# Where the plain part's last product stands, and which words and sums take a PSUM bank

## The chip, the cores and the metric

The kernel runs on one core of one Trainium2 chip. The metric is the device time of one execution in microseconds (us). Before the change it is 564.85 us, the median of three runs (564.38 to 565.11).

## The reference

The program chains three blocks in 32-bit floats. First a decaying linear attention over 2 batches, 8 heads, 768 positions and head size 64, in blocks of 64 positions with a running state. Its result, 1536 tokens by 512 features, goes through two feed-forward layers:

```python
rms = np.sqrt(np.mean(x * x, axis=-1, keepdims=True) + 1e-06)
xn = x / rms * rms_g
g = xn @ w_gate                                   # 512 x 1536
val = xn @ w_val                                  # 512 x 1536
x = (g * (1.0 / (1.0 + np.exp(-g))) * val) @ w_out            # 1536 x 512
h = np.maximum(np.maximum(x @ w1, x @ w2), x @ w3)            # 512 x 768 each
out = h @ w_out2                                  # 768 x 512
```

## The kernel before

**Split numbers.** Every operand of a large matmul is held as two parts, a high one (`wh`, `xh`, `hh`) and the remainder (`wl`, `xl`, `hl`). One product of a 128 x 128 weight tile with 512 columns is three matmuls: high by high, high by low, low by high.

**Tiles.** The 1536 tokens are three blocks of 512 columns, j = 0, 1, 2. Each weight unit is 128 x 512 words: `("g", f)`, `("v", f)` and `("o", f)` for hidden tile f = 0 to 11 of the first layer, `("1", f)`, `("2", f)`, `("3", f)` and `("p", f)` for f = 0 to 5 of the second.

**Two ways of multiplying.** Hidden tiles f = 0 to 5 are the plain part: `first_stage` goes through (group, j, f) in 18 steps, each with `hidden1` (gate and value products, 24 matmuls) and then `finish`, the output product of the step before, delayed by one step: four acc banks, 12 matmuls in `out1`, and at the last f of a group `drain1` (L456), four VectorE adds that bring the banks into `acc_sb`. From f = 6 on, `second_stage` computes the three column blocks by a scheme of fewer products: sums and differences of quarters of the inputs (names `s1` to `s4`, `11`, `12`, `22`, `2`) are multiplied by weight units and by pair sums of them. A work list names its pieces as `(at, n)`. `piece` makes 6 matmuls for one of them in tile p, q, r or p2, and `out_pair` 6 for an output tile acc. The `finish` of the last plain step is left over by the first stage and stands in this list: between `(at, (0, 1))` and `(at, 2)` of f = 6.

**The weight pipeline.** Raw words come by DMA on SP's queue (L149). A unit is made in cycles of three turns (`third_of_unit`), and `gap()`, called after each piece and twice in `finish`, makes one turn. Turn 0 begins a new unit (`begin_unit`: the load of a later one, two ScalarE passes L227 and L228, tile W) and makes the first step of the unit begun before: L188, VectorE, into tile `mid`. Turn 1 finishes the unit before that (cast to `wh` on ScalarE, L157; `wl` on GpSimd, L160) and makes L191 on `mid`. Turn 2 makes L194 on VectorE and L196 on GpSimd, which brings the result into W. `mid` is W itself in the first stage and a PSUM bank in the second.

**Pair sums.** A key with T (`("Tg", f)`, `("Tv", f)`, `("T1", f)` and so on) is a unit made from two finished ones, without a load. The first of a pair (`first_sum`) needs a copy of its partner's words in a PSUM bank, tile `tsum` (L181, ScalarE). Four half-width VectorE subtractions (L203) turn W and tsum into both sums. The second (`second_sum`) is finished straight from tsum: cast L157, and `wl` by VectorE, L173. The copy is made by `copy_partner` in turn 1 of the cycle ahead of that of the subtractions, which are spread over turns 0, 1 and 2 of their cycle as 2, 1, 1.

**Banks and order.** One pool of eight PSUM banks serves acc, p, q, r, p2, mid, tsum and the tiles of the first stage. A new tile takes the bank that was released first in program order, and waits for that bank's last reader. Each engine runs its instructions in the order of the program text; the kernel has no planner (`manual_schedule`).

**Quarter sums.** After the last output products of block j = 1 in the first layer, `sums_of_quarters` makes the second layer's inputs from the acc banks: two groups of VectorE L540, ScalarE casts L547, VectorE and GpSimd L447. It sets `quiet`, and no turn of the weight pipeline runs until `loud` in the work list, which stands after the output products of block j = 2 and the first pieces of the second layer.

Of the kernel before, what the change touches and what calls it, by code (L numbers as in the profile page):

```python
# [9 lines left out]
F32 = mybir.dt.float32  # L10
# [16 lines left out]
def tile_decay_attention_swiglu_maxout(  # L27
# [112 lines left out]
    mid = {}  # L140
    sums_in = {}
    room = [WBUFS, 8]
    pos = {"load": 0, "made": 0, "raw": 0, "step": 0, "gap": 0, "quiet": False, "lag": 3}

    def load_to(n):
        while pos["load"] < min(n, len(raw_list)):
# [5 lines left out]

    def finish_unit(key, W, at):
        if key:
            wh = wpools[at].tile([P, 512], F32R, tag="wh", name="wh")
            wl = wpools[at].tile([P, 512], F32R, tag="wl", name="wl")
            nc.scalar.copy(out=wh, in_=W.bitcast(F32))  # L157
            if second_sum(key):
                return lambda: lower_of_sum(key, W, wh, wl)
            nc.gpsimd.tensor_tensor(out=wl, in0=W.bitcast(F32), in1=wh.bitcast(F32), op=ALU.subtract)  # L160
            units[key] = (wh, wl)

    def first_sum(key):
        return key and (key[0] == "Tg" or key[0] != "Tv" and key[0][0] == "T" and key[1] % 2 == 0)

    def second_sum(key):
        return key[0][0] == "T" and not first_sum(key)

    def partner(key):
        return ("v", key[1]) if key[0] == "Tg" else (key[0][1], key[1] + 1)  # L170
# [2 lines left out]
        nc.vector.tensor_tensor(out=wl, in0=W.bitcast(F32), in1=wh.bitcast(F32), op=ALU.subtract)  # L173
        units[key] = (wh, wl)

    def copy_partner():
        if stage1 and first_sum(stage1[-1][0]):
            other = partner(stage1[-1][0])
            if other not in sums_in:
                sums_in[other] = psum.tile([P, 512], I32, tag="bank", name="tsum")  # L180
                nc.scalar.copy(out=sums_in[other].bitcast(F32), in_=words[other].bitcast(F32))  # L181

    def words_of_unit(n, key, W, at, lo, hi):

        if key and lo is not None:
            if n == 0:
                mid[key] = W if pos["step"] < len(steps) else psum.tile([P, 512], I32, tag="bank", name="mid")
                nc.vector.tensor_scalar(out=mid[key].bitcast(F32), in0=W.bitcast(F32), scalar1=LEAST, scalar2=MOST,  # L188
                                        op0=ALU.max, op1=ALU.min)
            elif n == 1:  # L190
                nc.vector.tensor_scalar(out=mid[key], in0=mid[key], scalar1=0x07FFFFFF, scalar2=3,  # L191
                                        op0=ALU.bitwise_and, op1=ALU.logical_shift_left)
            else:
                nc.vector.scalar_tensor_tensor(out=W, in0=hi, scalar=-0x40000000, in1=mid.pop(key),  # L194
                                               op0=ALU.bitwise_and, op1=ALU.bitwise_or)
                nc.gpsimd.tensor_tensor(out=W, in0=W, in1=lo, op=ALU.add)  # L196
        elif first_sum(key):
            a, b = W.bitcast(F32), sums_in[partner(key)].bitcast(F32)
            kept = words[partner(key)].bitcast(F32)
            todo = ((a[:, :HF], b[:, :HF], a[:, :HF]), (b[:, :HF], b[:, HF:], kept[:, :HF]),  # L200
                    (b[:, HF:], b[:, HF:], a[:, :HF]), (a[:, HF:], a[:, HF:], b[:, HF:]))
            for o, x, y in todo[(0, 2, 3)[n]:(2, 3, 4)[n]]:
                nc.vector.tensor_tensor(out=o, in0=x, in1=y, op=ALU.subtract)  # L203

    def begin_unit():
        if pos["made"] == len(unit_list):
            return
        key = unit_list[pos["made"]]
        at = group_of[key] % 2
        if first_use[key] <= pos["step"] + (6 if pos["step"] < 18 else 9) and at < len(wpools) and (key is None or room[at]):  # L210
            pos["made"] += 1
            if key is None:
                stage1.append((None,) * 5)
                return
            room[at] -= 1
            held[key] = at
            if key[0][0] == "T":
                stage1.append((key, (sums_in if second_sum(key) else words)[key[0][1], key[1]], at, None, None))
                return
            load_to(pos["raw"] + (3 if pos["step"] else 1))  # L220
            pos["raw"] += 1
            t = raws.pop(key).rearrange("p k (f w) -> p (k f) w", w=2)
            lo, hi = t[:, :, 0], t[:, :, 1]
            spare = key[0] in "12" and key[1] % 2
            W = (lates[0] if spare else wp).tile([P, 512], I32, tag="W", name="W", bufs=1 if spare else 3)
            words[key] = W
            nc.scalar.activation(out=W.bitcast(F32), in_=hi.bitcast(F32), func=AF.Abs)  # L227
            nc.scalar.activation(out=lo, in_=lo.bitcast(U32), func=AF.Copy, scale=2.0 ** -29)  # L228
            stage1.append((key, W, at, lo, hi))
# [14 lines left out]
    def third_of_unit():  # L244

        if not thirds:
            done = stage2.pop(0) if stage2 else (None,) * 3
            unit = stage1.pop(0) if stage1 else (None,) * 5
            later = []
            thirds.extend([lambda: (begin_unit(), words_of_unit(0, *unit)),  # L250
                           lambda: (later.append(finish_unit(*done)), copy_partner(), words_of_unit(1, *unit)),
                           lambda: (later[0] and later[0](), words_of_unit(2, *unit), stage2.append(unit[:3]))])
        thirds.pop(0)()

# [579 lines left out]
            third_of_unit()  # L834

    def second_stage(finish):
        def loud():
            pos["quiet"] = False
            third_of_unit()


        work = []
        before = None
        for f in range(PLAIN, F1):
            at = f, None
            outs = [[], [], []]
            if f == PLAIN:
                outs[1] = [finish]
            elif (f - PLAIN) % 2 == 0:
                outs = [out_block(f - 2, j) for j in (0, 2, 1)]  # L850
            work.append((at, 1))
            if before:
                work.append((before, 4))
            before = at
            if f == F1 - 1:
                work += [(at, n) for n in (5, 6, (0, 0), 2, 7, 3, (0, 1), (1, 0), 4)]
            else:
                work += [(at, 5), (at, (0, 0))] + outs[0] + [(at, 6), (at, (0, 1))] + outs[1] + [(at, 2)] + outs[2]
                work += [(at, n) for n in (3, 7, (1, 0), (1, 1))]
        first, second, third = (0, 0), (0, 1), (0, 2)  # L860
        work += out_block(F1 - 2, 0) + [(at, (1, 1))] + out_block(F1 - 2, 1) + [(first, 1), (first, 2), (second, 1)]
        work += out_block(F1 - 2, 2) + [loud]
        work += [(first, n) for n in (5, 6)] + [(second, 2)] + [(first, n) for n in (3, 7, (0, 0), (0, 1), (1, 0), 4, (1, 1))]
        work += [(second, n) for n in ((0, 0), (0, 1), 5, (1, 0), 6, 3, 7)] + [(third, 1), (second, (1, 1)), (second, 4)]
        work += [(third, n) for n in (2, (0, 0), (0, 1), (1, 0), 5, (1, 1), 6, 3)]
        at = 1, 0
        work += [(at, 1), (third, 7), (at, 2), (at, (0, 0)), (third, 4)] + [(at, n) for n in ((0, 1), 5, (1, 0), (1, 1), 6, 3)]
        outs = [lambda j=j, t=t: out2(0, j, t) for j in range(NBLK) for t in range(NB // P)]
        work += outs[:2] + [(at, 7)] + outs[2:4] + [(at, 4)] + outs[4:]
        before = None  # L870
        for g in range(F2 // 2):
            for i in range(3):
                at = g, i
                if at <= (1, 0):
                    continue
                if before:
                    work += [(at, 1), (before, 4)]
                else:
                    work.append((at, 1))
                work += [(at, n) for n in (5, (0, 0), 6, (0, 1), 2, 3, 7, (1, 0), (1, 1))]  # L880
                before = at
                if g and i == 0:
                    outs = [lambda g=g, j=j, t=t: out2(g - 1, j, t) for j in range(NBLK) for t in range(NB // P)]
                    work += outs[:2] + [(at, 4)] + outs[2:]
                    before = None
        work.append((before, 4))
        work += [lambda g=F2 // 2 - 1, j=j, t=t: out2(g, j, t) for j in range(NBLK) for t in range(NB // P)]
        for w in work:
            if callable(w):
                w()  # L890
            else:
                piece(*w)
# [66 lines left out]
```

## Time and profile before

| | before |
|---|---|
| median of three timed runs | 564.85 us |
| the profiled execution | 567.43 us |
| its span, first to last instruction | 564.5 us |
| TensorE matmuls (PE) | 547.1 us busy, 97%, 2880 |
| VectorE (DVE) | 383.1 us, 68%, 583 |
| GpSimd (POOL) | 320.7 us, 57%, 256 |
| ScalarE (ACT) | 272.0 us, 48%, 517 |
| mean granted TensorE clock | 0.989 |

The profile is of one execution. Times in rows are us from the start of the span. A row of the timeline gives start and duration, engine, line, operation, the tile written <- the tiles read, shapes, and in brackets how long the engine stood idle before it and whose end released it. Matmuls are pipelined, so their durations overlap, and the distance of their starts tells the pace. A granted clock of 1.00 is 2.4 GHz, 0.50 is 1.2 GHz.

### The profile page before, as it was taken

The numbers are of one execution on the slowest core, as the hardware profiler recorded it, in microseconds if no ns is written. First come the engines' busy times: TensorE is split into PE (matmuls) and PEld (weight loads), VectorE is DVE, ScalarE is ACT, GpSimd is POOL, SyncE is SP. The second block draws the span as 40 slices with busy tenths as digits, with TensorE's granted clock in tenths as the row PEclk, the third lists the DMA queues.
The fourth block names the chain that finished last, engine by engine and source line by source line (L and its number), as shares of the span: only waits on it lengthen the run. The fifth ranks groups of instructions, "written<-read, shape, count | busy, mean of one in ns | idle before, by whom it ended". The sixth has DMA issues, their size and how long they took to land.

```text
span 564.5 us, 7794 instructions
## 1 busy us (share of the span) xinstructions
PE 547.1 (97%) x2880; PEld 452.0 (80%) x2880; DVE 383.1 (68%) x583; ACT 272.0 (48%) x517; POOL 320.7 (57%) x256
## 2 busy tenths in 40 slices
PE   7979989999999999989999999999999999999997
PEld 7968767888788888778888888878888888888885
DVE  6687997423358789686676867896567567774364
ACT  3566754332354534446626455555465755552120
POOL 2577998311167677647727747687377553962050
PEclk9998999999999999989999999999999999999999
DMA  8767646000023211212312222120222322210014
GB/s 204 189 177 188 176 134 168 1 0 1 2 81 107 72 40 35 66 48 76 113 38 74 75 74 76 37 75 1 74 75 76 96 91 75 74 39 0 2 45 178
DMA packets 64646, 44.54 MB, mean 79 GB/s; under 512 B 39264, under 2 KB 60768, under 8 KB 64608
## 3 DMA queue, kind: packets, MB, share of 16 engines
q1 hardware_dynamic: 63936, 44.05, 26.6%
q8 instruction: 22, 0.36, 0.3%
q14 instruction: 16, 0.13, 0.1%
q10 hardware_dynamic: 672, 0.01, 0.1%
HBM read 40.90 MB, written 3.15 MB: 78 GB/s over the span
## 4 chain that ended last, share of the span: by engine, by line
PE 83%; DVE 9%; DMA 2%; ACT 2%; issue 1%; POOL 1%; SPq 0%; ACTq 0%; DVEq 0%
PE p L637 27%; PE r L637 7%; PE acc L425 5%; PE acc L427 5%; PE acc L426 5%; PE q L637 4%; PE acc L820 3%; PE acc L819 3%; PE acc L821 3%; PE pg L425 3%; PE pg L426 3%; PE pg L427 2%; PE pv L425 2%; PE pv L427 2%; PE pv L426 2%; PE px L322 2%
## 5 line engine op out<-in xcount | busy, mean ns | idle before, releaser
L160 POOL TENSOR_TENSOR wl<-W,wh 128x512 fp32r<-128x512 f32 x75 | 102.8, 1371 | 43.4 <-ACT wh L157 43.3
L196 POOL TENSOR_TENSOR W<-W,wraw 128x512 int32<-128x512 int32 x60 | 80.7, 1346 | 72.6 <-DVE W L194 70.8
L157 ACT CAST wh<-W 128x512 fp32r<-128x512 f32 x75 | 46.5, 620 | 68.0 <-POOL W L196 67.8
L439 POOL TENSOR_TENSOR hl<-sg,hh 128x512 fp32r<-128x512 f32 x36 | 48.8, 1356 | 43.5 <-ACT hh L438 43.5
L425 PE MATMUL acc<-hh,wh 128*128 128x512 f32 x144 | 57.2, 397 | 1.0 <-DVE xl L447 1.0
L426 PE MATMUL acc<-hl,wh 128*128 128x512 f32 x144 | 56.2, 390 | 0.0
L427 PE MATMUL acc<-hh,wl 128*128 128x512 f32 x144 | 56.1, 390 | 0.0
L637 PE MATMUL p<-xl,wh 128*128 128x512 f32 x120 | 46.7, 389 | 0.0
L637 PE MATMUL p<-xh,wh 128*128 128x512 f32 x120 | 46.7, 389 | 0.0
L637 PE MATMUL p<-xh,wl 128*128 128x512 f32 x120 | 46.7, 389 | 0.0
L227 ACT ACTIVATE W<-wraw 128x512 f32<-128x512 f32 x60 | 40.0, 667 | 9.6 <-POOL wl L160 5.6
L438 ACT CAST hh<-sg 128x512 fp32r<-128x512 f32 x36 | 22.3, 620 | 43.6 <-DVE sg L572 37.4
L228 ACT ACTIVATE wraw<-wraw 128x512 int32<-128x512 uint32 x60 | 39.7, 661 | 0.0
L439 POOL TENSOR_TENSOR hl<-m,hh 128x512 fp32r<-128x512 f32 x18 | 24.5, 1366 | 24.2 <-ACT hh L438 24.1
L637 PE MATMUL p<-yh,wh 128*128 128x512 f32 x90 | 35.0, 389 | 0.0
L637 PE MATMUL p<-yl,wh 128*128 128x512 f32 x90 | 35.0, 389 | 0.0
L637 PE MATMUL p<-yh,wl 128*128 128x512 f32 x90 | 35.0, 389 | 0.0
L692 ACT COPY c<-p 128x512 f32<-128x512 f32 x30 | 17.7, 588 | 33.5 <-PE p L637 33.4
L425 PEld LDWEIGHTS acc<-hh,wh 128*128 128x128 f32 x144 | 27.0, 188 | 7.5 <-DVE xl L447 1.8
L792 DVE TENSOR_TENSOR acc_sb<-acc,acc_sb 128x512 f32<-128x512 f32 x34 | 23.3, 690 | 14.1 <-PE acc L427 13.3
L188 DVE TENSOR_SCALAR mid<-W 128x512 f32<-128x512 f32 x37 | 25.4, 686 | 9.3 <-ACT W L227 4.7
L427 PEld LDWEIGHTS acc<-hh,wl 128*128 128x128 f32 x144 | 27.0, 188 | 5.8
(177 smaller groups left out, 1444.2 us busy)
## 6 DMA issues: line engine op xcount, KB each, us to landing
wraw<-in_moe_w_out_dram SPq DMA_DIRECT2D x18, 512.0 KB, 3.4
wraw<-in_moe_w_dram SPq DMA_DIRECT2D x18, 512.0 KB, 3.6
wraw<-in_moe_w_gate_dram SPq DMA_DIRECT2D x12, 512.0 KB, 3.6
wraw<-in_moe_w_val_dram SPq DMA_DIRECT2D x12, 512.0 KB, 3.6
kn<-in_k_dram SPq DMA_DIRECT2D x12, 256.0 KB, 4.1
qn<-in_q_dram SPq DMA_DIRECT2D x12, 256.0 KB, 4.4
vn<-in_v_dram SPq DMA_DIRECT2D x12, 256.0 KB, 4.7
out_dram<-acc_sb SPq DMA_DIRECT2D x12, 256.0 KB, 2.0
```

The source lines that it names most:

```text
L157: nc.scalar.copy(out=wh, in_=W.bitcast(F32))
L160: nc.gpsimd.tensor_tensor(out=wl, in0=W.bitcast(F32), in1=wh.bitcast(F32), op=ALU.subtract)
L188: nc.vector.tensor_scalar(out=mid[key].bitcast(F32), in0=W.bitcast(F32), scalar1=LEAST, scalar2=MOST, op0=ALU.max, op1=ALU.min)
L196: nc.gpsimd.tensor_tensor(out=W, in0=W, in1=lo, op=ALU.add)
L227: nc.scalar.activation(out=W.bitcast(F32), in_=hi.bitcast(F32), func=AF.Abs)
L228: nc.scalar.activation(out=lo, in_=lo.bitcast(U32), func=AF.Copy, scale=2.0 ** -29)
L425: nc.tensor.matmul(out=out, lhsT=wh, rhs=xh_, start=first, stop=False)
L426: nc.tensor.matmul(out=out, lhsT=wh, rhs=xl_, start=False, stop=False)
L427: nc.tensor.matmul(out=out, lhsT=wl, rhs=xh_, start=False, stop=last)
L439: nc.gpsimd.tensor_tensor(out=dst_l, in0=src, in1=dst_h.bitcast(F32), op=ALU.subtract)
L637: nc.tensor.matmul(out=ps, lhsT=w[:, ks], rhs=r[:, o + k, :], start=first and k == 0 and n == 0, stop=k == 1 and n == 2, skip_group_check= ...
L792: nc.vector.tensor_tensor(out=ps if kept else y, in0=ps, in1=y, op=ALU.add)
```

## The change

Three things change. The leftover `finish` stands ahead of `(at, (0, 1))` of f = 6 instead of behind it. `mid` stays W until the new work item `wide`, right after that piece, where before it became a bank at the beginning of the second stage. And the copy of a partner into tsum is made by `sum_bank` in turn 0 of the pair's own cycle, where before it was made two turns earlier; the four subtractions are spread over the turns as 0, 2, 2, and the second sum looks up its tile when it is finished instead of when it is begun.

```diff
     def finish_unit(key, W, at):
         if key:
+            if second_sum(key):
+                W = sums_in.pop((key[0][1], key[1]))
...
-    def copy_partner():
-        if stage1 and first_sum(stage1[-1][0]):
-            other = partner(stage1[-1][0])
-            if other not in sums_in:
-                sums_in[other] = psum.tile([P, 512], I32, tag="bank", name="tsum")
-                nc.scalar.copy(out=sums_in[other].bitcast(F32), in_=words[other].bitcast(F32))
+    def sum_bank(key):
+        other = partner(key)
+        sums_in[other] = psum.tile([P, 512], I32, tag="bank", name="tsum")
+        nc.scalar.copy(out=sums_in[other].bitcast(F32), in_=words[other].bitcast(F32))
...
-                mid[key] = W if pos["step"] < len(steps) else psum.tile([P, 512], I32, tag="bank", name="mid")
+                mid[key] = W if pos["narrow"] else psum.tile([P, 512], I32, tag="bank", name="mid")
...
         elif first_sum(key):
+            if n == 0:
+                sum_bank(key)
+                return
...
-            for o, x, y in todo[(0, 2, 3)[n]:(2, 3, 4)[n]]:
+            for o, x, y in todo[2 * n - 2:2 * n]:
                 nc.vector.tensor_tensor(out=o, in0=x, in1=y, op=ALU.subtract)
...
-                           lambda: (later.append(finish_unit(*done)), copy_partner(), words_of_unit(1, *unit)),
+                           lambda: (later.append(finish_unit(*done)), words_of_unit(1, *unit)),
...
+        def wide():
+            pos["narrow"] = False
...
             if f == PLAIN:
-                outs[1] = [finish]
+                work += [(at, n) for n in (1, 5, (0, 0), 6)] + [finish, (at, (0, 1)), wide]
+                work += [(at, n) for n in (2, 3, 7, (1, 0), (1, 1))]
+                before = at
+                continue
```

## Rows read from the trace of the kernel before

**Rows 1.** The page: busy us, share of the span, instructions of TensorE.
```profile
PE 547.1 (97%) x2880; PEld 452.0 (80%) x2880; DVE 383.1 (68%) x583; ACT 272.0 (48%) x517; POOL 320.7 (57%) x256
```

**Rows 2.** Stages from the seam on: length, engines' busy us, granted clock, DMA.
```profile
239.70:241.70 2.00, 0.04 (x1) 0.00 (x0) 1.32 (x3) 2.00 (x5) 1.19 (x2) 1.00 0.30 123
241.70:245.50 3.80, 3.78 (x10) 2.97 (x11) 2.77 (x5) 1.03 (x3) 0.52 (x1) 0.55 0.00 0
245.50:374.00 128.50, 128.50 (x568) 106.21 (x566) 95.49 (x151) 66.20 (x121) 80.96 (x62) 1.00 0.22 70
374.00:382.00 8.00, 7.01 (x30) 5.32 (x30) 7.84 (x14) 7.12 (x15) 7.08 (x6) 1.00 0.21 67
382.00:545.00 163.00, 163.00 (x721) 135.02 (x720) 103.84 (x171) 80.10 (x145) 88.01 (x69) 1.00 0.16 52
```

**Rows 3.** Waits of TensorE from 150 us on: total us, times, longest.
```profile
PE q L637 <- DVE acc_sb L456: 2.0, 1, 2.0
PE acc L425 <- DVE xl L447: 1.0, 1, 1.0
```

**Rows 4.** Timeline of TensorE at the seam, single matmuls.
```profile
235.47 0.39 PE L637 MATMUL p<-xh,wh 128*128 128x512 f32 x1
...
237.09 0.39 PE L426 MATMUL acc<-hl,wh 128*128 128x512 f32 x1
...
239.35 0.39 PE L427 MATMUL acc<-hh,wl 128*128 128x512 f32 x1
241.72 0.60 PE L637 MATMUL q<-xh,wh 128*128 128x512 f32 x1 [1.98 <-DVE acc_sb L456]
...
245.47 0.39 PE L637 MATMUL r<-zh,wh 128*128 128x512 f32 x1
```

**Rows 5.** Timeline of VectorE at the seam.
```profile
240.38 0.70 DVE L188 TENSOR_SCALAR mid<-W 128x512 f32<-128x512 f32 x1 [4.63 <-ACT sg L713]
240.98 2.48 DVE L456 TENSOR_TENSOR acc_sb<-acc,acc_sb 128x512 f32<-128x512 f32 x4
```

**Rows 6.** Timeline of ScalarE at the seam.
```profile
237.65 0.62 ACT L157 CAST wh<-W 128x512 fp32r<-128x512 f32 x1 [3.25 <-POOL W L196]
...
239.78 0.57 ACT L713 ACTIVATE sg<-p 128x512 f32<-128x512 f32 x1
```

**Rows 7.** Timeline of GpSimd at the seam: the low part for `finish`.
```profile
233.37 1.74 POOL L439 TENSOR_TENSOR hl<-sg,hh 128x512 fp32r<-128x512 f32 x1
```

**Rows 8.** Timeline of TensorE at the quarter sums.
```profile
373.79 0.39 PE L637 MATMUL p<-yh,wl 128*128 128x512 f32 x1
...
378.17 0.50 PE L425 MATMUL acc<-hh,wh 128*128 128x512 f32 x1 [0.99 <-DVE xl L447]
...
381.06 0.39 PE L637 MATMUL r<-xh,wh 128*128 128x512 f32 x1
```

**Rows 9.** Timeline of VectorE and ScalarE at the quarter sums.
```profile
373.42 1.41 DVE L447 TENSOR_TENSOR xl<-acc,xh 128x512 fp32r<-128x512 f32 x2
...
377.42 1.41 DVE L447 TENSOR_TENSOR xl<-acc,xh 128x512 fp32r<-128x512 f32 x2
378.75 0.68 DVE L657 TENSOR_TENSOR m<-q,c 128x512 f32<-128x512 f32 x1
...
369.63 0.58 ACT L181 COPY tsum<-W 128x512 f32<-128x512 f32 x1
...
380.06 2.54 ACT L438 CAST yh<-acc_sb 128x512 fp32r<-128x512 f32 x4
```

**Rows 10.** Lines 188, 191, 194 from SBUF to SBUF: count, ns least/median/most.
```profile
L188 DVE TENSOR_SCALAR W<-W x23: 409/488/1514, 24.9 to 230.4; 128x512 f32<-128x512 f32 x23
...
L191 DVE TENSOR_SCALAR W<-W x23: 410/606/1520, 25.4 to 231.6; 128x512 int32<-128x512 int32 x23
...
L194 DVE SCALAR_TENSOR_TENSOR W<-wraw,W x23: 679/1486/1776, 26.6 to 232.3; 128x512 int32<-128x512 int32 x23
```

**Rows 11.** Waits of ScalarE from 245 us on: total us, times, longest.
```profile
ACT wh L157 <- POOL W L196: 53.8, 23, 5.8
```

More of the change, by code (lines that the diff above doesn't have):

```diff
@@ L142, in tile_decay_attention_swiglu_maxout @@
     room = [WBUFS, 8]
-    pos = {"load": 0, "made": 0, "raw": 0, "step": 0, "gap": 0, "quiet": False, "lag": 3}
+    pos = {"load": 0, "made": 0, "raw": 0, "step": 0, "gap": 0, "quiet": False, "lag": 3, "narrow": True}
     def load_to(n):
@@ L217, in begin_unit @@
             if key[0][0] == "T":
-                stage1.append((key, (sums_in if second_sum(key) else words)[key[0][1], key[1]], at, None, None))
+                stage1.append((key, None if second_sum(key) else words[key[0][1], key[1]], at, None, None))
                 return
```

## The prediction

> **What bounds the kernel now.** I read the page first: TensorE is busy 547.1 of 564.5 us [rows 1]. So time can come only from TensorE's own idle stretches, from a stretch at the lower clock, or from less work, and the change takes no matmul away (12 + 6 + 6 stand in another order). Next the stages: from 245.5 to 374 us and from 382 to 545 us TensorE is busy for the whole stretch, 128.50 of 128.50 and 163.00 of 163.00; between lie two places where it is not [rows 2]. The list of who waited for whom names both and, after 150 us, no third: q's first matmul waited 2.0 us for VectorE's add L456, and an acc matmul waited 1.0 us for VectorE's L447 [rows 3].
>
> The first place is the seam that the diff touches. In the steady stretches a 512-column matmul takes 0.226 us (128.50 us by 568, 163.00 by 721) [rows 2]. The last product of the plain part starts at 239.35, q's first one at 241.72, and six matmuls of q and four of r bring it to 245.47 [rows 4]. These are 10 steps, 2.26 us at the steady pace, and they took 6.12: 3.86 us are lost. Of these 2.14 are the wait (2.37 less one step). The other 1.72 are the clock: granted 0.55 from 241.7 to 245.5, 1.2 GHz for nearly all of it, against 1.00 while TensorE stood and again from 245.5 on (3.80 x 0.45 = 1.71) [rows 2].
>
> Why did q wait? The bank pool gives a new tile the bank whose last reader stands earliest in program order. At the seam eight banks are taken: four acc, p, r, the pair's copy tsum, and p2. The word stage of the next unit (g of f = 8) asks for one more, mid, and gets p2's, which is free only after the Silu L713. VectorE stands 4.63 us at L188 for it, and the four acc drains L456, one of which frees q's bank, stand behind it, from 240.98 [rows 5]. The Silu was late as ScalarE stood 3.25 us at a cast for GpSimd's W, and ran at 239.78 [rows 6].
>
> **The change part by part.**
> *finish before (f 6, (0, 1)), mid in SBUF.* What moves: 12 matmuls, two gaps with their turns of the weight pipeline, four L456 adds and a release. They now stand ahead of six matmuls of p2. The mid of g 8 no longer asks for a bank, and its turn falls behind the drains. Then: finish starts at 235.47, where the six p2 matmuls started [rows 4]. Its second matmul needs hl, at 235.70 instead of 237.09; GpSimd ends hl at 233.37 + 1.74 = 235.11 [rows 7], so the cover shrinks from 1.98 to 0.59 us but holds. Finish ends its 12 starts at 238.19, p2's six at 239.55, q is due then. Its bank is that of the first acc, whose three matmuls are through by about 236.3; one L456 is a quarter of the 2.48 us that four take [rows 5], so the bank is free at about 237.0, 2.5 us early. Ahead of L456 on VectorE stand only the pair's four half-width subtractions, whose copy on ScalarE comes before the cast that waits for GpSimd. So nothing late is left in front of q: gain 3.86 us, the clock included, as TensorE no longer stands still ahead of q. Bounds: 0 (q still waits as long) to 3.86.
>
> What moves along: the turn that begins v of f 8 (two ScalarE passes, one 512 KB load on SP's queue) comes one piece later; that load waits for a raw buffer anyway and its unit is due more than ten pieces on. What is late next at the seam is ScalarE, still held by the cast for GpSimd [rows 6]: Silu of p2, casts and the Silu of q follow each other from 240.3 on, and only VectorE's products wait for them.
>
> *mid in SBUF, the price.* Three VectorE steps of one unit now run from SBUF to SBUF. In the first stage these took 0.41 to 1.51 (L188), 0.41 to 1.52 (L191) and 0.68 to 1.78 us (L194) [rows 10]; with mid in a bank L188 took 0.70 [rows 5], and I use that for all three, 2.1 us. So the three cost between -0.6 and +2.7 us of VectorE's time. I take 0 for TensorE: GpSimd has little to do then, and the banks wanted next are the other three acc, drained by 239. The Trainium skill (SBUF — State Buffer, Who interferes with whom) says that a VectorE instruction with two SBUF inputs, or in a two-port mode, and one of GpSimd that reads SBUF shut each other out for a whole instruction. It speaks against this edit; the upper ends just given look like it. By the rule the cost is the +2.7, and it is a rival below.
>
> *The copy of a pair's sum in its own turn.* Per pair: the same ScalarE copy and the same four subtractions; the copy asks for its bank two turns later, the subtractions run as 0, 2, 2 instead of 2, 1, 1, all done in the same third turn. It frees a bank two turns longer per pair. Where TensorE never waited, that gains nothing. At one place it does: the quarter sums at 374 to 382 us. There turns are suspended, and the copy of the pair (1, 0), (1, 1) was made just before, at 369.63 [rows 9], so it sat on a bank through the whole stage. In the new order it comes behind the four acc of the last block, and each of these is one bank better off: the third gets the bank of the block before's second acc instead of its third, the fourth that of the third. Now from p's last start at 373.79 to r's first at 381.06 stand 25 steps, 5.65 us at the steady pace, and they took 7.27: 1.62 lost [rows 8]. New: acc 1, 2 and 3 start at 374.02, 375.38 and 376.74 without a wait (their banks are free by 374.83, the end of the first pair of L447); acc 4, due at 378.10, waits for the first of the two L447 of 377.42, through at about 378.12. Six steps, and the 0.18 us that a halt costs on top (the 12 steps from 378.17 to 381.06 took 2.89 us), bring r to 379.66. Its own bank waits for L657, 378.75 + 0.68 = 379.43 [rows 9], in time. Gain 381.06 - 379.66 = 1.40.
>
> Against it: the copy now stands on ScalarE behind the four casts that end at 382.60 and ahead of the copies out of r and p. 382.60 + 0.58 for it and 0.58 for r's gives 383.76; r's second half is due three pieces (4.07 us) after 379.66, at 383.73. I take 0.1 us for that, 1.3 net; bounds 0 (the copy comes as early as before) to 1.6.
>
> Elsewhere I take 0: TensorE has no wait from 382 to 545 us [rows 2], everything there hangs on it and moves with it; to the side of a loss the bound is the slower rival.
>
> **Sum.** 3.86 + 1.3 = 5.2 us. The profiled execution took 567.43 us for a span of 564.5, 2.9 around it, 2.6 above the median of the timed runs, 564.85. Its span becomes 559.3 and the execution 562.2; from the median 564.85 - 5.2 = **559.7 us**. The range of this case alone is 559.0 to 560.8.
>
> **The rivals.**
> *Only the seam gains* (12%). The quarter sums are held by VectorE itself: from 374 to 382 us it is busy 7.84 of 8.00 us [rows 2]; a bank sooner would not help if r still came late. Against: the work that needed these sums is r, and its inputs come at 378.8. Time 564.85 - 3.86 = 561.0.
> *A wait of about 2.7 us in its place* (8%). VectorE's three steps at their longest, or hl 0.6 us and more later than before, and TensorE stops again at the seam, at full price. 559.7 + 2.7 = 562.4. For it: VectorE is saturated up to 230 us and hl hangs on its chain. Against: 2.5 us of cover at q. The rule of the Trainium skill above (SBUF — State Buffer) is this case if GpSimd happens to be in all three steps' way.
> *No change* (5%). q's bank hangs on something that stays, or the shift is eaten by loads or GpSimd further on: 564.8. Against: GpSimd stood idle 4.09 of the 5.80 us from 239.7 to 245.5 us (busy 1.19 and 0.52) [rows 2], so its backlog does not carry over.
> *Slower* (5%): the pair's subtractions stop VectorE. The copy comes one turn before them instead of two, and ScalarE stands up to 5.8 us at the cast for GpSimd's W (23 times, 53.8 us in all) [rows 11]. If the copy fell behind such a halt, VectorE would stand at L203, drains would queue behind it as they do now behind L188, where 4.63 us of VectorE cost 3.86 of TensorE. Fifteen pairs are summed; from two such halts on the kernel is slower: 564.85 - 5.2 + 2 x 3.86 = 567.4. Against: the copy stands ahead of the next unit's cast, behind the same one as before, so it is late only where it was late already.
>
> **How the numbers follow.** The main case has 70%, the four rivals 12, 8, 5 and 5. The range from 558.8 to 562.3 holds the main case, the first rival and the beginning of the second, a good 80%. A measurement of this kernel tells 0.2%, 1.1 us, from no change: faster covers the main case and the first two rivals, 0.89 with a little taken off for what lies between; same 0.06, slower 0.05.
>
> **What would show it.** At the seam: q follows p2 without idle, a granted clock of 1.00 from 239 to 246 us, L188 as W<-W once more, the four L456 between 236 and 239.1 us, no wait of VectorE for the Silu L713. At the quarter sums: the copy L181 not at 369 but after the four yh casts; TensorE's wait for L447 down from 1.0 to about 0.1 us; r about 1.4 us closer to p. Wrong, if a wait of TensorE at the seam is left with the clock at half, if the acc of the last block still waits 1 us, or if L203 shows VectorE waiting for L181 in many pairs and TensorE for VectorE behind it.

## The result and the profile after

The changed kernel takes 560.23 us (median of 6 runs, 559.83 to 562.01). Runs of the kernel before on the same chip took 564.98 us (564.38 to 567.22). The ratio, after to before, is 0.9913, 95% interval 0.9891 to 0.9935; it is that of the means (565.35 and 560.45 us) and not quite that of the medians. By the medians the kernel is faster by 4.75 us, where 5.2 were predicted (559.7 us, range 558.8 to 562.3). The profiled execution took 560.53 us with a span of 558.6, where that of before took 567.43 with 564.5. That difference, 6.9 us, is larger than the medians' because the execution of before on record was one of its longer ones; below it turns out why they differ.

The page after, busy time of each engine:

```profile
PE 544.2 (97%) x2880; PEld 449.6 (80%) x2880; DVE 381.7 (68%) x583; ACT 272.1 (49%) x517; POOL 321.3 (58%) x256
```

The other engines do what they did [rows 1]; TensorE is busy 2.9 us less with the same 2880 matmuls; the stretch at the lower clock that is gone is part of it. The stages after, in the columns of [rows 2] (length, busy us of TensorE, its weight loads, VectorE, ScalarE and GpSimd, granted clock, DMA):

```profile
235.40:239.60 4.20, 4.20 (x20) 3.46 (x20) 3.72 (x5) 2.97 (x6) 3.85 (x4) 1.00 0.41 125
239.60:245.50 5.90, 5.90 (x28) 4.89 (x27) 4.74 (x9) 3.85 (x8) 2.48 (x2) 1.00 0.00 0
245.50:370.00 124.50, 124.50 (x551) 103.10 (x550) 91.72 (x145) 64.64 (x119) 79.58 (x61) 1.00 0.24 73
370.00:378.00 8.00, 8.00 (x36) 6.29 (x35) 7.13 (x12) 7.22 (x15) 7.68 (x7) 1.00 0.16 54
...
382.00:541.00 159.00, 159.00 (x703) 131.68 (x702) 101.10 (x166) 76.87 (x139) 85.75 (x66) 1.00 0.17 53
```

What these rows show: TensorE is busy in the whole of each stretch, at a granted clock of 1.00. Where [rows 2] had 0.04 of 2.00 us at the seam, a clock of 0.55 behind it and 7.01 of 8.00 at the quarter sums, there is no hole left; the list of TensorE's waits from 150 us on, two lines in [rows 3], is empty.

The seam. Line numbers are three higher than before in most of the kernel (L456 is L459, L713 is L716, L637 is L640). TensorE, single matmuls (start, length, line, tile):

```profile
234.78 0.39 PE L428 MATMUL acc<-hh,wh 128*128 128x512 f32 x1
235.01 0.39 PE L429 MATMUL acc<-hl,wh 128*128 128x512 f32 x1
...
237.28 0.39 PE L430 MATMUL acc<-hh,wl 128*128 128x512 f32 x1
...
238.86 0.39 PE L640 MATMUL q<-xh,wh 128*128 128x512 f32 x1
...
240.90 0.39 PE L640 MATMUL r<-zh,wh 128*128 128x512 f32 x1
```

VectorE at the same place:

```profile
235.66 2.73 DVE L459 TENSOR_TENSOR acc_sb<-acc,acc_sb 128x512 f32<-128x512 f32 x4 [0.82 <-PE acc L430]
238.41 0.98 DVE L188 TENSOR_SCALAR W<-W 128x512 f32<-128x512 f32 x1
240.42 0.70 DVE L756 TENSOR_TENSOR q<-q,c 128x512 f32<-128x512 f32 x1 [1.03 <-PE q L640]
241.03 0.42 DVE L191 TENSOR_SCALAR W<-W 128x512 int32<-128x512 int32 x1
...
242.99 0.68 DVE L194 SCALAR_TENSOR_TENSOR W<-wraw,W 128x512 int32<-128x512 int32 x1
```

The drains run at 235.66, as soon as the first product is summed, instead of behind a step that stood 4.63 us for the Silu [rows 5]. q follows without a pause. From the first of these 28 steps to r's fourth matmul (finish's products, p2, q, r, in whichever order) it is 240.90 - 234.78 = 6.12 us; before, from 235.47 to 245.47, it was 10.00 [rows 4]. The gain is 3.88 us.

The quarter sums, TensorE and then VectorE and ScalarE:

```profile
369.20 0.39 PE L640 MATMUL p<-yh,wl 128*128 128x512 f32 x1
...
373.58 0.50 PE L428 MATMUL acc<-hh,wh 128*128 128x512 f32 x1
...
375.09 0.39 PE L640 MATMUL r<-xh,wh 128*128 128x512 f32 x1
...
379.20 0.39 PE L640 MATMUL r<-xh,wh 128*128 128x512 f32 x1
```

```profile
372.83 1.41 DVE L450 TENSOR_TENSOR xl<-acc,xh 128x512 fp32r<-128x512 f32 x2
...
378.48 0.42 DVE L206 TENSOR_TENSOR W<-tsum,W 128x256 f32<-128x256 f32 x1 [1.25 <-ACT tsum L181]
```

```profile
375.47 2.41 ACT L441 CAST yh<-acc_sb 128x512 fp32r<-128x512 f32 x4
377.79 0.58 ACT L181 COPY tsum<-W 128x512 f32<-128x512 f32 x1
378.31 0.58 ACT L695 COPY c<-r 128x512 f32<-128x512 f32 x1
```

From p's last start to r's first it is 5.89 us where it was 7.27 [rows 8]: 1.38 gained. The copy L181 now stands behind the four casts; the fourth acc starts 0.08 us late (373.58, due at 373.50).

3.88 and 1.38 are 5.26 of the 5.9 us between the spans. The other 0.7 lie ahead of the seam (its first step at 235.47 before, 234.78 after), in a stretch that differs between executions of one kernel: in the three traces of the kernel before that there were in the end q starts at 241.72, 240.67 and 240.44. The granted clock from 30 to 60 us, in the attention part, was 0.89 in the first of them and 1.00 in the other two (0.94 in the trace of after).

### The profile page after: what moved, and what is told of

Its sections match the earlier page's. It is cut to its first block, busy times and chain, and to the rows that moved or that the text cites. A ratio compares the mean times of both kernels' runs of the same rounds, so it can differ in the third digit from the quotient of the medians.

```text
span 558.6 us, 7798 instructions
## 1 busy us (share of the span) xinstructions
PE 544.2 (97%) x2880; PEld 449.6 (80%) x2880; DVE 381.7 (68%) x583; ACT 272.1 (49%) x517; POOL 321.3 (58%) x256
## 4 chain that ended last, share of the span: by engine, by line
PE 89%; DVE 5%; POOL 2%; issue 1%; DMA 1%; ACT 0%; SPq 0%; POOLq 0%; DVEq 0%; ACTq 0%
PE p L640 29%; PE r L640 7%; PE acc L428 6%; PE acc L430 6%; PE acc L429 6%; PE q L640 4%; PE acc L824 3%; PE acc L822 3%; PE acc L823 3%; PE pv L428 3%; PE pg L428 3%; PE pv L430 3%; PE pv L429 3%; PE pg L430 3%; PE pg L429 3%; PE px L325 2%
## 5 line engine op out<-in xcount | busy, mean ns | idle before, releaser
L640 PE MATMUL p<-xh,wh 128*128 128x512 f32 x120 | 46.7, 389 | 0.0
L640 PE MATMUL p<-xl,wh 128*128 128x512 f32 x120 | 46.7, 389 | 0.0
L640 PE MATMUL p<-xh,wl 128*128 128x512 f32 x120 | 46.7, 389 | 0.0
L442 POOL TENSOR_TENSOR hl<-m,hh 128x512 fp32r<-128x512 f32 x18 | 24.5, 1366 | 24.0 <-ACT hh L441 23.9
L640 PE MATMUL p<-yh,wh 128*128 128x512 f32 x90 | 35.0, 389 | 0.0
L640 PE MATMUL p<-yl,wh 128*128 128x512 f32 x90 | 35.0, 389 | 0.0
L640 PE MATMUL p<-yh,wl 128*128 128x512 f32 x90 | 35.0, 389 | 0.0
L428 PE MATMUL pv<-xh,wh 128*128 128x512 f32 x72 | 29.7, 413 | 2.0 <-DVE x L381 2.0
```

The lines of the kernel that those rows point to most:

```text
L428: nc.tensor.matmul(out=out, lhsT=wh, rhs=xh_, start=first, stop=False)
L442: nc.gpsimd.tensor_tensor(out=dst_l, in0=src, in1=dst_h.bitcast(F32), op=ALU.subtract)
L640: nc.tensor.matmul(out=ps, lhsT=w[:, ks], rhs=r[:, o + k, :], start=first and k == 0 and n == 0, stop=k == 1 and n == 2, skip_group_check= ...
```

## The experiments

Each kernel was timed beside the kernel before; of the third trace of before there is one execution only. The first four experiments split the change. A ratio is that of this kernel's time to before's, with its 95% interval.

**The output products alone.**

```diff
-                outs[1] = [finish]
+                work += [(at, n) for n in (1, 5, (0, 0), 6)] + [finish, (at, (0, 1))]
+                work += [(at, n) for n in (2, 3, 7, (1, 0), (1, 1))]
+                before = at
+                continue
```

> The kernel before with finish ahead of (0, 1) alone; mid asks for a bank as before, sums as before. My theory: mid's turn now falls behind the drains, so it gets the first acc's bank and q the second's, both drained 2 us before they are wanted; no wait at the seam: 564.98 - 3.9 = 561.1 us, the same as with mid in W. Rival (mid must be out of the banks): mid still waits for the Silu or takes q's bank, q waits 1 to 2 us, 562.5 to 564.9 us.

Measured 561.87 us (12 runs), ratio 0.9949, 0.9929 to 0.9968; 0.8 above the expectation, with two heaps of runs (more under "What stays open"). No wait at the seam: TensorE is busy for 8.00 of the 8.00 us from 238 to 246 us. One wait is left after 150 us:

```profile
PE acc L425 <- DVE xl L447: 0.9, 1, 0.9
```

**The products and the words, without the pair's new place.** The edit above and these lines.

```diff
-                mid[key] = W if pos["step"] < len(steps) else psum.tile([P, 512], I32, tag="bank", name="mid")
+                mid[key] = W if pos["narrow"] else psum.tile([P, 512], I32, tag="bank", name="mid")
...
+                work += [(at, n) for n in (1, 5, (0, 0), 6)] + [finish, (at, (0, 1)), wide]
```

> The kernel before with two parts of the change: finish stands ahead of (0, 1) and mid stays in W until wide; the copy of a pair's sum keeps its old place. My theory (two separate losses): the seam gives its 3.9 us, the quarter sums stay: 564.98 - 3.9 = 561.1 us; TensorE's wait for L447 is 1.0 us as before and its wait for L456 is gone. Rival (the sum's bank is needed at the seam too, since the copy would hold the eighth bank): q still waits, 564.9 us.

Measured 561.53 us (11 runs), ratio 0.9945, 0.9927 to 0.9962. It is no different from the products alone; the wait of 1.0 us for L447 stays here as well.

**The words alone.**

The line on `pos["narrow"]` as above, and finish in its old place.

```diff
-                outs[1] = [finish]
+                outs[1] = [finish, wide]
```

> The kernel before with mid kept in W until right behind finish, finish in its old place behind (0, 1), sums as before. VectorE is then not held at L188, the drains L456 follow finish at once. My theory (banks go out in the order in which they were released in the program): q now gets the bank of p2, which the Silu L713 reads until about 240.4 us, so q waits 0.8 us there; the clock, which stayed at 1.00 through the 1.0 us halt at the quarter sums, stays up: 564.98 - 3.9 + 0.8 = 561.9 us. Rival A (mid in a bank was the whole cause): 561.1 us, no wait. Rival B (drains behind the last product are too late for q wherever mid lies, so finish has to move): 564.5 us and more.

Measured 563.08 us (12 runs), ratio 0.9968, 0.9950 to 0.9986: 1.2 us above what I expected. At q the mechanism is the expected one; on VectorE it is not. TensorE, then VectorE:

```profile
239.26 0.50 PE L637 MATMUL q<-xh,wh 128*128 128x512 f32 x1 [0.69 <-ACT sg L713]
```

```profile
238.28 0.98 DVE L188 TENSOR_SCALAR W<-W 128x512 f32<-128x512 f32 x1 [3.67 <-ACT W L227]
239.19 2.47 DVE L456 TENSOR_TENSOR acc_sb<-acc,acc_sb 128x512 f32<-128x512 f32 x4
```

With mid gone from the banks q itself gets p2's, waits 0.69 us for the Silu. VectorE, which I had expected to be free, is still held at L188, 3.67 us, now for ScalarE's pass L227, so that the drains come as late as before; but they hold up nobody. The wait is 1.3 us shorter, and the lowest run (562.24) lies 1.2 us under the lowest of before (563.47). What I had counted on beside that was the clock's 1.7 us, in every run of the kernel before.

**The pair's place alone.** The third part of the change and nothing else; its core:

```diff
+            if n == 0:
+                sum_bank(key)
+                return
...
-            for o, x, y in todo[(0, 2, 3)[n]:(2, 3, 4)[n]]:
+            for o, x, y in todo[2 * n - 2:2 * n]:
```

> The kernel before with the third part alone: the copy of a pair's sum is made in its own turn, the subtractions run as 0, 2, 2. My theory: at the seam all eight banks are still taken, mid still gets p2's bank, q waits 2 us and the clock falls, and only the quarter sums gain: 564.98 - 1.4 = 563.6 us; the copy at the quarter sums comes behind the four yh casts. Rival (the copies' time in banks counts at many of the 15 pairs, the seam among them): 561.5 us or less, with q's wait shortened.

Measured 561.96 us (12 runs), ratio 0.9953, 0.9936 to 0.9969. A miss: it gained 3.0 us, not 1.4. The quarter sums' wait is gone, as expected; the surprise is at the seam, TensorE and then its windows:

```profile
239.85 0.50 PE L640 MATMUL q<-xh,wh 128*128 128x512 f32 x1 [1.65 <-DVE acc_sb L459]
```

```profile
238.00:239.80 1.80, 0.20 (x1) 0.00 (x0) 1.29 (x3) 1.80 (x4) 0.99 (x2) 1.00 0.20 80
239.80:243.60 3.80, 3.75 (x16) 3.11 (x17) 3.74 (x7) 2.12 (x5) 0.55 (x1) 1.00 0.00 0
```

The wait is still there, 0.3 us shorter (the rival had said shorter, but why by this much was not looked into), and the clock does not fall behind it. So two of my four expectations failed by the same term. That opened the question that the remaining runs were for: does the clock fall at the seam in every execution of the kernel before?

**The kernel before, traced again.** No edit.

> The kernel before, unchanged, once more with a trace of its own. Open is whether TensorE's clock falls behind the seam's wait in every execution: the trace on record shows a wait of 1.98 us and then a granted clock of 0.55 for 3.8 us, and the run with only the third part kept its wait of 1.65 us without any fall. If the fall belongs to the kernel, it is here again, with a wait of q near 2.0 us, a profiled time 2 to 3 us above the median of runs, and span near 564.5. If it comes in some executions only, the clock is 1.00 here from 240 to 246 us, q waits 1.6 to 2.0 us, and the profiled time is near 565.0 or below, 1.7 us or more under the first trace's 567.4. Time against itself: ratio 1.000.

Measured 564.08 us (11 runs, 563.59 to 566.67); beside it the same kernel took 565.67 (16 runs). The ratio of this kernel to itself came out as 0.9981, 0.9967 to 0.9996: with 11 and 16 runs such an interval can miss one, and I read no difference under 0.3% from one comparison. The seam in this trace, TensorE and its windows:

```profile
240.67 0.50 PE L637 MATMUL q<-xh,wh 128*128 128x512 f32 x1 [2.00 <-DVE acc_sb L456]
...
242.85 0.39 PE L637 MATMUL r<-zh,wh 128*128 128x512 f32 x1
```

```profile
238.50:240.60 2.10, 0.17 (x1) 0.00 (x0) 1.26 (x3) 2.10 (x5) 1.27 (x2) 1.00 0.29 119
240.60:244.50 3.90, 3.83 (x17) 3.17 (x18) 3.84 (x8) 2.21 (x5) 0.57 (x1) 1.00 0.00 0
```

The same kernel, the same wait (2.00 against 1.98), and no fall. The fall comes in some executions only. In this and the other comparisons there were 82 timed executions of the kernel before; their spans lie in two heaps: 38 from 561.5 to 562.6 us, 44 from 563.1 to 566.2, nothing between. The heaps' means are 562.0 and 564.2. A fall such as that of the trace on record lowers the mean granted clock of an execution by 0.003 (0.45 x 3.8 of 564.5 us). Of the 44 upper executions none has a mean clock above 0.997; of the 38 lower ones 15 have 0.999 or 1.000. That is what it would look like if every upper execution had a fall, and it does not say where in the execution.

**A third trace of it**, one execution, run last.

> The kernel before once more, for a third trace. The 82 timed executions so far lie in two heaps by their span, 38 up to 562.6 us and 44 from 563.1 us on, and the two traces are one of each: 564.5 with the clock at 0.55 behind q's wait, 561.8 without. If the fall behind the seam's wait is what parts the heaps, a span of 563.1 or more here comes with a granted clock well below 1.00 in the 4 us behind q's wait, and a span of 562.6 or less with 1.00 there. If a long span comes with 1.00 there, the heaps have another cause.

The span was 563.2. TensorE and its windows:

```profile
240.44 0.50 PE L637 MATMUL q<-xh,wh 128*128 128x512 f32 x1 [2.03 <-DVE acc_sb L456]
...
244.06 0.53 PE L637 MATMUL r<-zh,wh 128*128 128x512 f32 x1
```

```profile
237.00:240.40 3.40, 1.41 (x7) 0.83 (x5) 1.30 (x3) 3.40 (x7) 2.57 (x3) 1.00 0.44 154
240.40:241.00 0.60, 0.56 (x2) 0.48 (x3) 0.60 (x2) 0.60 (x2) 0.54 (x1) 0.94 0.00 0
241.00:244.40 3.40, 3.40 (x9) 2.63 (x8) 2.48 (x4) 0.82 (x3) 0.00 (x0) 0.51 0.00 0
244.40:250.00 5.60, 5.60 (x26) 4.59 (x25) 4.91 (x9) 2.21 (x4) 2.22 (x2) 1.00 0.06 15
```

The upper heap, and the fall is there, this time from 241.0 to 244.4 us. From q's first matmul to r's fourth it is 3.62 us, against 2.18 in the trace without a fall: 1.44 us more, and the spans differ by 1.4. In both traces the clock is 1.00 everywhere else up to 555 us. So the fall accounts for the longer span, within the 0.2 us by which q starts earlier here.

**A longer wait.** Before, with three multiplications by 1.0 on VectorE ahead of the four drains.

```diff
                     if f == f1:
+                        if (g, j) == (1, NBLK - 1):
+                            for _ in range(3):
+                                nc.vector.tensor_scalar(out=acc[3], in0=acc[3], scalar1=1.0, scalar2=1.0,
+                                                        op0=ALU.mult, op1=ALU.mult)
                         drain1(acc, g, j)
```

> The kernel before with three multiplications by 1.0 of the fourth output product's bank on VectorE between the next set's first narrow step and the four drains of the last plain block, so that q, which still takes the first product's bank, waits about 2.2 us longer: some 4.2 us in place of 2.0 (three steps of 0.73 us). It tests what decides on the fall of TensorE's clock behind that wait. So far runs of the kernel before fall into two heaps, and of two traces with waits of 1.98 and 2.00 us one shows the fall and one doesn't. If it hangs on the wait's length, nearly every run here has it: the lowest runs are at 563.5 + 2.2 + 1.7 = 567.4 us, there is one heap at the seam, and the profile shows a granted clock below 0.7 behind the wait. If the length has no part in it, the heaps stay two, the lowest runs near 565.7 us.

Measured 569.21 us (11 runs, 567.29 to 571.42), ratio 1.0059, 1.0033 to 1.0084. TensorE and its windows:

```profile
245.12 0.79 PE L641 MATMUL q<-xh,wh 128*128 128x512 f32 x1 [4.09 <-DVE acc_sb L456]
...
249.12 0.63 PE L641 MATMUL r<-zh,wh 128*128 128x512 f32 x1
```

```profile
240.80:245.10 4.30, 0.23 (x2) 0.00 (x0) 3.31 (x6) 2.98 (x6) 1.93 (x2) 0.79 0.18 71
245.10:250.00 4.90, 4.88 (x12) 3.81 (x13) 3.06 (x5) 1.18 (x3) 0.00 (x0) 0.50 0.00 0
```

Here the clock falls while TensorE still stands, and the lowest run is at 567.29, where I expected 567.4 with a fall in every run and 565.7 without. No run lies near the lower figure, and none of the 11 has a mean granted clock above 0.993. So by the times every execution has the fall here; one of them was traced. With the third part alone (1.65 us) nine of the 12 spans, 559.6 to 560.2, leave no room for a fall of 1.4 us, and three, 560.9 to 561.6, do. This fits an account in which a longer wait has the fall in more of the executions, and in about half of them at the 2.0 us of the kernel before; three lengths do not show it.

**A wait put into the kernel after.** The same multiplications, four and six of them, ahead of its drains, meant to bring back waits of 1.9 and 3.1 us.

```diff
+                        if (g, j) == (1, NBLK - 1):
+                            for _ in range(4):
+                                nc.vector.tensor_scalar(out=acc[3], in0=acc[3], scalar1=1.0, scalar2=1.0,
+                                                        op0=ALU.mult, op1=ALU.mult)
                         drain1(acc, g, j)
```

> The kernel after, with four multiplications by 1.0 of the fourth output product's bank on VectorE ahead of the four drains of the last plain block: the bank that q takes then comes free at about 240.8 us where q is due at 238.9, so q waits some 1.9 us again (estimate: 4 x 0.6 us from 237.7, and one drain). Nothing else is changed and the result is the same. If a wait of this length costs its length alone, TensorE loses 1.9 us: 562.1 us against 560.2 (562.4 with what a second wait on VectorE may add). If the clock falls behind such a wait as in the first trace of before, it is 1.7 us more: 563.8 us.

> The kernel after with six such multiplications in place of four: q is released at about 242.0 us, a wait of some 3.1 us. Length alone: 563.3 us. With a fall of the clock to 0.55 for 3.8 us behind it: 565.0 us, and the windows show the granted clock below 0.7 in the stretch right behind the wait.

Measured 562.15 us (5 runs, 561.01 to 562.98) and 561.25 us (4 runs, 561.11 to 561.37). The experiment did not do what it was made for. TensorE with four, and VectorE's drains there; then TensorE with six:

```profile
240.28 0.50 PE L644 MATMUL q<-xh,wh 128*128 128x512 f32 x1 [0.86 <-ACT sg L720]
...
240.91 2.47 DVE L459 TENSOR_TENSOR acc_sb<-acc,acc_sb 128x512 f32<-128x512 f32 x4
```

```profile
239.38 0.50 PE L644 MATMUL q<-xh,wh 128*128 128x512 f32 x1 [0.85 <-ACT sg L720]
```

q starts before the first drain does, so it has none of the four acc banks: with the drains later, the pool gave it p2's, and q waited 0.86 us for the Silu whatever VectorE did. That also corrects the rule for the pool: in the text of the kernel the drains stand ahead of the Silu as they do in after, and the multiplications release nothing, yet q's bank is another. So the order of release by which the pool goes is not that of the text alone; what it goes by was not looked into. What is left is the price of such a wait: with six, 1.0 us, at a clock of 1.00 behind it. The 1.9 us of the other are not explained by its seam. In its trace q starts 0.9 us later than with six, for the same wait, so the difference lies ahead of the seam, where the clock from 30 to 60 us was 0.89 against 0.94; its five runs are scattered over 2 us, and that their median lies on the 562.1 expected for a wait of 1.9 us is chance.

**The quarter sums alone undone.** The kernel after, in which one pair's copy is made a turn early, where it stood before.

```diff
+    def early_pair():
+        if stage1 and stage1[-1][0] == ("T2", 0) and partner(("T2", 0)) not in sums_in:
+            sum_bank(("T2", 0))
...
             if n == 0:
-                sum_bank(key)
+                if partner(key) not in sums_in:
+                    sum_bank(key)
                 return
...
-                           lambda: (later.append(finish_unit(*done)), words_of_unit(1, *unit)),
+                           lambda: (later.append(finish_unit(*done)), early_pair(), words_of_unit(1, *unit)),
```

> The kernel after, but the one pair whose copy stood ahead of the quarter sums before takes its bank there again, one turn early; all other pairs and the seam are as after. So only the part of the change that bears on the quarter sums is undone. My theory prices it at 1.4 us less 0.1: the sums' third output product of block 3 waits about 1.0 us on VectorE's quarter sum again, and TensorE's stretch of 25 steps from p to r takes 7.3 us where it took 5.9: 561.6 us. The rival, from the run of the third part alone that gained 3.0 us: 563.2 us, if the pair's place alone is worth 3.0.

Measured 561.88 us (6 runs), 1.65 above after where 1.3 to 1.4 were expected. The wait is back, and the stretch from p to r is 7.25 us (369.50 to 376.75):

```profile
369.50 0.39 PE L645 MATMUL p<-yh,wl 128*128 128x512 f32 x1
...
373.88 0.50 PE L433 MATMUL acc<-hh,wh 128*128 128x512 f32 x1 [0.98 <-DVE xl L455]
...
376.75 0.39 PE L645 MATMUL r<-xh,wh 128*128 128x512 f32 x1
```

By the trace the stretch is 1.36 us longer than after. So the place of this one pair, of fifteen, carries all that this part of the change was priced at.

**The words back in a bank.** The kernel after with `wide` ahead of the first piece instead of behind the seam.

```diff
-                work += [(at, n) for n in (1, 5, (0, 0), 6)] + [finish, (at, (0, 1)), wide]
+                work += [wide] + [(at, n) for n in (1, 5, (0, 0), 6)] + [finish, (at, (0, 1))]
```

> The kernel after, but the words of the two units around the seam take a bank of PSUM for their narrow steps, as before; the moved output products and the pair's new place stay. My theory, with the run in which only the output products moved: the place of the words is worth nothing once the products stand ahead, so 560.2 us, the same as after, no wait at the seam. Rival, if the words in SBUF carry part of the gain: q waits up to 2 us, 561 to 562.2 us.

Measured 560.15 us (6 runs, 559.74 to 560.89), ratio 0.9913, 0.9883 to 0.9942: the same as after, and TensorE has no wait from 150 us on. The trace has 37 sets of words in a bank where after has 36, so it is the words of one unit that moved, not of two as I had written. Their place is worth nothing once the products stand ahead.

**All words in SBUF.** The kernel after with the narrow steps kept to the end.

```diff
         def wide():
-            pos["narrow"] = False
+            pos["narrow"] = True
```

> The kernel after with all later units' words kept in SBUF for their three steps on VectorE (36 further sets) instead of a bank of PSUM. In the plain part the same steps took between 0.41 and 1.77 us each beside GpSimd's work on SBUF, where the steps on a bank took 0.68 to 0.69. If the two engines hinder each other, VectorE is busy some 10 to 30 us longer and TensorE waits for late weights in places: 561 to 566 us. If not, or if nothing waits for VectorE there, the time is that of after within 0.3 us: 560.0 to 560.5 us.

Measured 563.02 us (12 runs, 562.44 to 566.08), 2.8 above after. The page, and TensorE's waits from 150 us on:

```profile
PE 542.8 (97%) x2880; PEld 447.9 (80%) x2880; DVE 406.6 (72%) x583; ACT 271.9 (48%) x517; POOL 331.5 (59%) x256
```

```profile
PE acc L428 <- DVE xl L450: 1.2, 2, 1.0
PE p L640 <- ACT c L695: 0.9, 1, 0.9
```

VectorE is busy 24.9 us longer and GpSimd 10.2, over 36 sets that do the same three steps. From 243.5 to 515 us these steps took, 36 times each, 27.9 (L188), 32.1 (L191) and 39.2 us (L194), against 24.7, 25.0 and 24.5 with the words back in a bank: L194, which now reads two tiles in SBUF, has more than half of the loss. TensorE gets 2.1 us of waits back, and the span is 2.3 longer. The Trainium skill (SBUF — State Buffer, Who interferes with whom) says that a VectorE instruction with two SBUF inputs, or in a two-port mode, and a GpSimd instruction that reads SBUF lock each other out for a whole instruction. These numbers agree with that; no run here separates it from another cause.

## Why the prediction was right, and where it was off

*The seam.* Right in mechanism and, in the profile, in size: 3.88 us against 3.86. q follows p2, the clock is 1.00, the drains run from 235.66 to 238.39 (236 to 239.1 was said), L188 is W<-W. The rule for the pool on which it rests is not the whole rule (the wait put into the kernel after), but at the seam it did not mislead. The term, however, was mis-sized as a mean. Of its two summands, wait and clock, the wait is paid in every execution of the kernel before, and the clock's 1.72 only in those with a fall: 1.57 us in the trace on record (3.75 from q to r's fourth, against 2.18 without a fall) and 1.44 in the third. The heaps fit the same account: 44 of 82 executions, 2.2 us longer on average than the others, put some 1.2 us on the mean. (The 2.2 are more than the fall's 1.5. The trace on record also has the clock of 0.89 from 30 to 60 us, where the third has 1.00; its q starts 1.28 us later and its span is 1.3 us longer. What else parts the heaps was not traced.) The lower heap's median span, 562.0, against 558.4 after, leaves 3.6: the always-paid part, from 2.3 at the seam (2.39 less a step between the last acc and q, and 0.14 of slow restart) and 1.38 at the sums. 3.6 + 1.2 = 4.8; the means are 4.9 apart, the medians 4.75. I took the clock's share from one execution and subtracted it from a median over both kinds; the 0.45 us by which the forecast missed are no more than six runs scatter, and that it came so close has luck in it: the median of the kernel before was 564.30 where 10 of 21 executions lay in the upper heap, 564.95 with 17 of 34, and 565.67 with 13 of 16. The term was sized wrongly all the same, and the experiments that I priced with it, the third part alone and the words alone, missed by 1.6 and 1.2 us. (The third part alone: 1.38 at the sums, 0.3 of q's wait and the 1.2 of the falls make 2.9 of the 3.0 us.)

*The words in SBUF.* Predicted price on TensorE 0, and it is 0. The three steps took 0.98 + 0.42 + 0.68 = 2.08 us, the 2.1 that I used. But the step itself was superfluous: the argument counted mid's bank among the causes, and the bank matters only while it stands ahead of the drains in VectorE's queue. The rival of a 2.7 us wait named a cost that is there when all words stay in SBUF (the last experiment); at the seam, where GpSimd has little to do, it did not come.

*The quarter sums.* 1.40 predicted, 1.38 found. The 0.1 us that I took off for the copy on ScalarE did not come: r's second half starts at 379.20 with no wait, its c having been made at 378.31 + 0.58 = 378.89. The rival "only the seam gains" is out: the two experiments on the pair's place show its own gain.

*The slower rival* came closer than the time shows. VectorE's wait at the subtractions for the pair's copy, in the kernel before and in the kernel after:

```profile
DVE W L203 <- ACT tsum L181: 1.2, 3, 0.5
```

```profile
DVE W L206 <- ACT tsum L181: 8.3, 5, 3.3
```

The wait that I feared is seven times as long in all and falls on five pairs. It costs TensorE nothing in this trace, which has no wait of TensorE after 150 us. "Late only where it was late already" was wrong for VectorE; that it does not matter was luck of the places, not shown by my argument.

**What stays open.** What decides in one execution whether the clock falls behind a wait of 2.0 us. By what order the pool hands out its banks. And of the five kernels that keep the 1 us wait at the sums, 6 of 53 executions are 2 to 3 us longer than their others (finish alone: three at 561.8 to 562.0 us of span, nine at 559.1 to 560.8). These six have mean granted clocks of 0.990 and 0.991, and all others of these kernels 0.992 or more, so a stretch at the lower clock goes with them; no trace fell on one, so I don't know where it lies.

## What to carry to other kernels

When a wait ends at the drain of a bank, look at which instruction is queued ahead of the drains on their engine, rather than at the bank: moving the producer forward cured both the wait and what hung on it, and keeping the words in SBUF beside it did nothing. After a change look up which bank the pool gave, as it may be another. Price a wait of the matmul engine by its length, plus the lower clock times the share of executions in which it falls, and get that share from the spans of many executions, not from the one that was traced. In this kernel a temporary that only VectorE reads was better off in a bank of PSUM where GpSimd works on SBUF at the same time: 36 sets of words moved to SBUF cost 2.8 us.

## What the runs showed of the hardware

TensorE's granted clock behind a stop, in the traces: 1.00 after 0.69, 0.86 and 1.65 us; after 2.00 us once 1.00, after 1.98 and 2.03 us 0.55 and 0.51 for the next 3.4 to 3.8 us; after 4.09 us down to 0.50 already before the engine started again. In the trace with 2.03 us the first two matmuls of q still ran at the full clock and the fall came 0.6 us after the restart: an engine that had resumed and did not stand again was slowed. At half clock the spacing of the 512-column matmuls was 0.43 us, at full clock 0.23.
